# Splitting the first loads, moving block 1's attention ahead of half a projection, and merging two stores at the end of a linear-attention and gated-FFN kernel

## The chip, the cores and the metric

The kernel runs on one core of a Trainium2 chip. The metric is the device time of one execution in microseconds (us), lower is better. The profile of one execution gives a span, from its first to its last instruction, about 2 us shorter than the time. PE is TensorE (the matmul engine), DVE is VectorE, ACT is ScalarE, POOL is GpSimd and SP is SyncE.

## The reference

Linear attention with a decay per head over blocks, then a gated feed-forward layer, in float32. Cut to what matters:

```python
# q, k, v: (4 batches, 8 heads, 768 positions, 64), lam: (8,)
for b in range(nb):                                    # blocks of positions
    intra = einsum('bhic,bhjc->bhij', qb, kb) * Dmask  # scores, decayed and causal
    intra = einsum('bhij,bhjd->bhid', intra, vb)
    inter = einsum('bhid,bhde->bhie', qb * lam_pow, kv_state)
    out[:, :, sl] = intra + inter
    kv_state = lam_block * kv_state + einsum('bhsd,bhse->bhde', kb * rev_pow, vb)
x = out.transpose(0, 2, 1, 3).reshape(3072, 512)
gate = 1 / (1 + exp(-(x @ w_gate)))                    # w_gate, w_val: (512, 1536)
return (gate * (x @ w_val)) @ w_out                    # w_out: (1536, 512)
```

## The kernel before

The kernel works through six blocks of 128 positions, each with all four batches. A block has three parts:

- Attention: transposes of k and q; scores (`sp`); mask products on VectorE (`MT`); the part from the state (`piece_i`) and the value part (`piece_a`), which add up in `op`; copies of these to `XT`; and the update of the state from k with its decays (`KD`, on ScalarE) and v.
- Gate/value: 12 tiles of 128 columns, each with four gate matmuls (`gp`) and four value matmuls (`vp`).
- Output projection (`po`): 12 matmuls over the 12 tiles, for each batch.

The attention of the next block is threaded into the matmul stream of the block that is running. All inputs are float32 and become bfloat16 on the way in; GpSimd issues those loads, one after the other. These are the lines that the change touches:

```python
    # first loads, block 0 (batches 0, 1 of k come by another way)
    load(0, "q", 0, 2)
    load(0, "k", 2, 4)
    load(0, "q", 2, 4)
    load(0, "v", 0, 2)
    load(0, "v", 2, 4)
    load_gv(0, 1); load_gv(1, 2); load_gv(2, 4); load_gv(4, 6)   # gate and value weights by tiles
    # ... cut: tables of decays
    load_gv(6, 8); load_gv(8, 12)
    load(1, "k", 0, 2); load(1, "q", 0, 2)
    load_wo(0, 256)                        # output weights, columns 0 to 255, all 12 row tiles
    load(1, "k", 2, 4); load(1, "q", 2, 4)
    load_wo(256, 512)
    load(1, "v")
    load(2, "kq")
```

(The statements joined by semicolons stand on lines of their own in the kernel.) Block 0's projection runs in two halves of 256 columns, with block 1's attention between the half projections:

```python
    behind[10] = [trans(1, 0)]                          # behind gate tile 10 of block 0
    behind[11] = [pair(piece_s, 1, 0), m_(1, 0)]
    # ...
    after = {(0, 0): [m_(1, 1)], (0, 1): [kd(1, 0), trans(1, 1)],
             (0, 2): [pair(piece_s, 1, 1), m_(1, 2), kd(1, 2)],
             (0, 3): [pair(piece_c, 0, 0), pair(piece_c, 0, 1), m_(1, 3)],
             (1, 0): [kd(1, 4)], (1, 1): [kd(1, 6)], (1, 2): [att(1)]}
    for j in range(2):
        for tt in range(B):
            po(0, tt, *after.get((j, tt), []), c=(256 * j, 256 * (j + 1)))
    # ... the last projection of the kernel (last block, last batch):
                po(n, tt, c=(0, 256))
                po(n, tt, c=(256, 384), eng=nc.vector)
                po(n, tt, c=(384, 512))
```

Each `po` ends with a copy out of PSUM (ScalarE, or VectorE where `eng` says so) and a store that SyncE issues.

## Time and profile before

| | before |
|---|---|
| time, median of the first 3 runs | 229.35 us (229.12 to 229.72) |
| span of the profiled run | 227.2 us |
| PE busy | 218.9 us (96%) |
| first gate matmul starts | 15.85 us |
| first projection matmul starts | 38.65 us |
| first gate matmul of block 1 | 54.09 us |

Busy time by stretches of the kernel before: the stretch in us and its length, then busy us and number of instructions of each engine, the granted clock, the DMA share and GB/s.

```profile
core 0: us, PE busy (x) PEld busy (x) DVE busy (x) ACT busy (x) POOL busy (x), PEclk, DMA share, GB/s
...
15.42:38.65 23.23, 22.55 (x132) 10.56 (x129) 10.25 (x16) 11.52 (x23) 13.47 (x14) 1.00 1.62 193
38.65:54.09 15.44, 15.27 (x260) 13.14 (x257) 9.40 (x18) 9.04 (x26) 4.64 (x5) 1.00 2.18 167
54.09:88.85 34.76, 34.76 (x275) 16.80 (x273) 17.34 (x35) 15.90 (x36) 13.89 (x17) 1.00 1.42 166
```

From 54.09 us on PE is full (34.76 of 34.76 us), so the change can act only on what lies ahead of that, and on the last store. PE is full at its rate too: matmuls of 512 columns start 0.216 us apart. That is what the Trainium skill gives in "TensorE: Matmul & The Clock Gate", section "Back-to-back issue gap", as the isolated gap of a warm array (512/2.4 + 2.5 ns = 216 ns).

PE's waits of 0.3 us and more between 12 and 60 us in the kernel before: who waited for whom, us in total, times, longest.

```profile
PE gp L336 <- ACT XT L421: 0.4, 1, 0.4
PE vp L342 <- DMA WV<-in_moe_w_val_dram: 0.3, 1, 0.3
```

How block 1's attention lies in the stream before is shown by PE's timeline: start, duration, line, operation, output and inputs, number.

```profile
46.57 4.10 PE L358 MATMUL po<-WO,ht 128*128 128x256 bf16 x36
50.61 0.64 PE L285 MATMUL op<-QS,Sb 64*64 64x128 bf16 x32
51.18 1.08 PE L296 MATMUL op<-MT,vb 128*64 128x128 bf16 x32
52.09 0.74 PE L314 MATMUL cp<-vb,kd 128*64 128x64 bf16 x32
52.77 1.48 PE L358 MATMUL po<-WO,ht 128*128 128x256 bf16 x12
54.09 1.03 PE L336 MATMUL gp<-XT,WG 128*128 128x512 bf16 x4
...
57.55 1.03 PE L336 MATMUL gp<-XT,WG 128*128 128x512 bf16 x4
```

The state part (50.61), the value part (51.18) and the state update (52.09) follow one another without a gap, because 36 projection matmuls, 4 us, stand between the update of block 0's state and them; VectorE has done its mask products by then. The last half projection (52.77) covers the copies to `XT` that the first gate matmul of block 1 (54.09, "gate 1" from here on) needs. The line at 57.55 is tile 2 of block 1's gates, counted from 0.

The end: ScalarE's last copy, and SyncE's last stores (its line merges four).

```profile
223.31 0.27 ACT L361 COPY ob<-po 128x128 f32<-128x128 f32 x1 [0.97 <-PE po L358]
```

```profile
221.27 2.88 SPq L350 DMA_DIRECT2D out_dram<-ob  x4
```

The last copy ends at 223.58, the span at 227.17.

The trace also has every load's landing on its semaphore. The ones that matter (us, last of the 16 engines): v of block 0's batches 2, 3 at 14.24, first half of the output weights 38.34, q of block 1's batches 2, 3 41.84, second half of the output weights 45.84, v of block 1 49.16.

### The profile page before, as it was taken

Reading aid. Unit: us, or ns where it says so; the run is one execution under the profiler, and the core shown is the slowest. Engines: PE = TensorE matmul, PEld = TensorE weight load, DVE = VectorE, ACT = ScalarE, POOL = GpSimd, SP = SyncE. Lnnn points to the kernel's source line nnn. Section 1 sums busy time; section 2 is a strip of 40 time slices with the busy share of each in tenths; the row PEclk is TensorE's granted clock in tenths of the full one; section 3 lists DMA queues with packets and bytes.
Section 4 is the critical chain, followed back from the end, with each engine's and each line's share of the span. In section 5 each row is a group of like instructions: output and inputs, shape, how many; then the busy total and the mean of one; then the engine's idle time right before and its main releaser. Section 6 shows DMA issues by size and latency. Waiting matters only on the chain.

```text
span 227.2 us, 4266 instructions
## 1 busy us (share of the span) xinstructions
PE 218.9 (96%) x1725; PEld 111.2 (49%) x1725; DVE 101.8 (45%) x186; ACT 101.2 (45%) x217; POOL 58.1 (26%) x73
## 2 busy tenths in 40 slices
PE   6789999999999999999999999999999999999993
PEld 2444436887444644444644444644444544444452
DVE  4764435547378610488420388430378400334200
ACT  5777433763328723348523338532422342433221
POOL 7997545600192039005800030000000000000000
PEclk9999999999999999999999999999999999999999
DMA  7999999999999929993992959012100012100022
GB/s 114 149 173 202 203 175 182 187 158 142 277 154 159 190 76 151 207 186 61 149 171 97 217 42 66 3 46 92 46 3 0 3 46 92 46 0 3 0 92 94
DMA packets 104708, 25.31 MB, mean 111 GB/s; under 512 B 94065, under 2 KB 101745, under 8 KB 104689
## 3 DMA queue, kind: packets, MB, share of 16 engines
q0 software_dynamic: 81760, 13.90, 78.8%
q1 hardware_dynamic: 22464, 11.01, 19.3%
q8 instruction: 13, 0.21, 0.4%
q10 hardware_dynamic: 464, 0.14, 0.4%
q14 instruction: 7, 0.05, 0.1%
HBM read 28.32 MB, written 6.29 MB: 152 GB/s over the span
## 4 chain that ended last, share of the span: by engine, by line
PE 84%; DMA 9%; POOL 4%; ACT 1%; issue 1%; POOLq 0%
PE po L358 27%; PE vp L342 24%; PE gp L336 24%; DMA WV<-in_moe_w_val_dram 6%; DMA vb<-in_v_dram 3%; PE sp L266 2%; PE op L296 2%; PE op L285 1%; PE cp L314 1%; POOL WV L105 1%; POOL WG L104 1%; POOL qb L92 1%; POOL vb L92 1%; ACT kd L120 1%; POOL kb L92 0%
## 5 line engine op out<-in xcount | busy, mean ns | idle before, releaser
L345 DVE TENSOR_TENSOR ht<-sg,vp 128x512 bf16<-128x512 bf16 x72 | 49.5, 687 | 96.9 <-PE vp L342 95.2
L336 PE MATMUL gp<-XT,WG 128*128 128x512 bf16 x288 | 74.0, 379 | 0.4 <-ACT XT L421 0.4
L342 PE MATMUL vp<-XT,WV 128*128 128x512 bf16 x288 | 73.9, 379 | 0.3 <-DMA WV<-in_moe_w_val_dram 0.3
L339 ACT ACTIVATE sg<-gp 128x512 bf16<-128x512 f32 x72 | 43.0, 597 | 65.6 <-PE gp L336 63.2
L358 PE MATMUL po<-WO,ht 128*128 128x512 bf16 (+2 forms) x360 | 64.1, 337 | 0.0
L358 PEld LDWEIGHTS <-ht 128*128 128x128 bf16 x360 | 33.5, 98 | 27.9
L342 PEld LDWEIGHTS <-WV 128*128 128x128 bf16 x288 | 28.0, 98 | 34.7 <-DMA WV<-in_moe_w_val_dram 1.2
L336 PEld LDWEIGHTS <-WG 128*128 128x128 bf16 x288 | 27.5, 98 | 32.7 <-issue 0.3
L361 ACT COPY ob<-po 128x512 f32<-128x512 f32 (+2 forms) x29 | 14.7, 507 | 46.4 <-PE po L358 46.4
L274 DVE TENSOR_TENSOR MT<-sp,mask 128x512 bf16<-128x512 f32 x48 | 30.6, 683 | 2.0 <-PE sp L266 2.0
L120 ACT ACTIVATE kd<-kb,kds 128x128 bf16<-128x128 bf16 (+1 forms) x72 | 23.8, 402 | 0.0
L443 POOL COPY gates<-kt 128x1 bf16<-128x1 bf16 x4 | 1.2, 304 | 52.1 <-DMA kt<-kb 52.1
L306 ACT CAST XT<-op 128x512 bf16<-128x512 f32 x21 | 10.9, 597 | 5.6 <-PE op L296 5.6
L92 POOL DMA_DIRECT2D vb<-in_v_dram x7 | 10.9, 1564 | 2.7 <-DMA kb<-in_k_dram 1.0
L323 DVE SCALAR_TENSOR_TENSOR Sb<-Sb,dec,cp 128x128 bf16<-128x128 bf16 x32 | 8.6, 342 | 3.3 <-PE cp L314 3.3
L98 POOL DMA_DIRECT2D kb<-in_k_dram x10 | 8.8, 892 | 3.7 <-DMA WO<-in_moe_w_out_dram 2.7
L98 POOL DMA_DIRECT2D qb<-in_q_dram x10 | 8.9, 906 | 2.1 <-DMA WG<-in_moe_w_gate_dram 1.7
L371 PE MATMUL zps<-Sb 128*128 128x512 bf16 x21 | 7.5, 482 | 1.5 <-DVE Sb L147 1.5
L92 POOL DMA_DIRECT2D qb<-in_q_dram x7 | 8.4, 1201 | 1.1 <-POOLq L560 0.8
L92 POOL DMA_DIRECT2D kb<-in_k_dram x6 | 7.0, 1158 | 0.7 <-DMA WG<-in_moe_w_gate_dram 0.7
L296 PE MATMUL op<-MT,vb 128*64 128x128 bf16 x184 | 6.5, 221 | 0.0
L296 PEld LDWEIGHTS <-vb 128*64 128x64 bf16 x184 | 5.3, 110 | 1.3 <-issue 0.4
(55 smaller groups left out, 79.9 us busy)
## 6 DMA issues: line engine op xcount, KB each, us to landing
out_dram<-ob SPq DMA_DIRECT2D x23, 256.0 KB, 2.0
vb<-in_v_dram POOLq DMA_DIRECT2D x5, 512.0 KB, 7.1
qb<-in_q_dram POOLq DMA_DIRECT2D x7, 256.0 KB, 7.5
kb<-in_k_dram POOLq DMA_DIRECT2D x6, 256.0 KB, 8.0
WO<-in_moe_w_out_dram POOLq DMA_DIRECT2D x2, 768.0 KB, 15.5
kb<-in_k_dram POOLq DMA_DIRECT2D x10, 128.0 KB, 9.5
qb<-in_q_dram POOLq DMA_DIRECT2D x10, 128.0 KB, 10.0
WG<-in_moe_w_gate_dram POOLq DMA_DIRECT2D x3, 256.0 KB, 8.3
```

The lines of the kernel that those rows point to most:

```text
L92: nc.gpsimd.dma_start(out=T_[c, n][:, b0:nat], in_=src[b0:nat, :, sl, :].rearrange("b h s d -> s (b h) d"))
L98: nc.gpsimd.dma_start(out=T_[c, n][:, m:b1, u::2, :], in_=src[m:b1, 1 - u::2, sl, :].rearrange("b h s d -> s (b h) d"))
L120: nc.scalar.mul(KD[n][:, at, i, :], T_["k", n][:, at, i, :], kds[:, h:h + 1])
L274: nc.vector.tensor_tensor(out=MT[n, b][:, u], in0=SP[n, b][u], in1=(mask if n else mask0)[:, 1 - u if swapped(n, b) else u], op=ALU.mult)
L296: nc.tensor.matmul(OP[n, b][rows_of(w), hp, :], lhsT=T_["v", n][:, b, h, :], rhs=MT[n, b][:, slot(n, b, h) % 2, hp, :], start=(n == 0 and ...
L306: (e.tensor_copy if e is nc.vector else e.copy)(XT[n][:, :, b, :], OP[n, b])
L336: nc.tensor.matmul(gp, lhsT=WG[:, mt, fs], rhs=x[:, mt, :], start=(mt == 0), stop=(mt == NMT - 1))
L339: nc.scalar.activation(sg, gp, AF.Sigmoid)
L342: nc.tensor.matmul(vp, lhsT=WV[:, mt, fs], rhs=x[:, mt, :], start=(mt == 0), stop=(mt == NMT - 1))
L345: nc.vector.tensor_mul(HT[n, ft], sg, vp)
L358: nc.tensor.matmul(po[:, :c1 - c0], lhsT=HT[n, ft][:, tt * 128:(tt + 1) * 128], rhs=WO[:, ft, c0:c1], start=(ft == 0), stop=(ft == NFT - 1))
L361: (eng.copy if eng is nc.scalar else eng.tensor_copy)(o, po[:, :c1 - c0])
```

## The change

The intent: let the scores of block 0's batches 2 and 3 start as soon as each batch's q is there; keep the weights arriving in step with the gate tiles; bring v of block 1 ahead of the second half of the output weights, so that attention 1 can run early and this half's projection moves into gate/value 1; and have one store fewer at the end. The core of the diff:

```diff
-    load(0, "q", 2, 4)
+    load(0, "q", 2, 3)
+    load(0, "q", 3, 4)
     load(0, "v", 0, 2)
-    load(0, "v", 2, 4)
-    load_gv(0, 1)
-    load_gv(1, 2)
-    load_gv(2, 4)
+    load(0, "v", 2, 3)
+    load(0, "v", 3, 4)
+    for ft in range(4):
+        load_gv(ft, ft + 1)
 ... (transposes may take a PSUM buffer of the other pool; so does block 1's op)
-    t_("k", 0, [2, 3])
-    e_k(0, [2, 3], parts=2)
+    for b in range(2, 4):
+        t_("k", 0, [b], ps_ff, "ff")
+    e_k(0, [2])
     piece_s(0, [1])
     piece_m(0, 1)
-    zeros(2)
     t_("q", 0, [2])
     e_q(0, [2], nc.scalar)
+    e_k(0, [3])
+    zeros(2)
     t_("q", 0, [3])
-    e_q(0, [3], nc.vector)
+    e_q(0, [3], nc.scalar)
 ... (scores of batches 2 and 3 one by one, other filler matmuls, XT of batch 2 on VectorE)
     load_gv(6, 8)
-    load_gv(8, 12)
+    nc.gpsimd.dma_start(out=WG[:, :, 8 * 128:], in_=wg_r[:, :, 8 * 128:])
+    for ft in (8, 10):
+        fs = slice(ft * 128, (ft + 2) * 128)
+        nc.gpsimd.dma_start(out=WV[:, :, fs], in_=wv_r[:, :, fs])
 ...
     load(1, "q", 2, 4)
+    load(1, "v", 0, 2)
+    load(1, "v", 2, 4)
     load_wo(256, 512)
-    load(1, "v")
     load(2, "kq")
 ...
-    behind[10] = [trans(1, 0)]
-    behind[11] = [pair(piece_s, 1, 0), m_(1, 0)]
+    behind[10] = [trans(1, 0), kd(1, 0, 2, parts=[0])]
+    behind[11] = [pair(piece_s, 1, 0), m_(1, 0), kd(1, 2, 4, parts=[0])]
 ... (the table "after" and its loop go)
+    po(0, 0, m_(1, 1), kd(1, 4, 6, parts=[0]), c=cols[0])
+    po(0, 1, pair(piece_c, 0, 0), pair(piece_c, 0, 1), kd(1, 6, 8, parts=[0]), c=cols[0])
+    po(0, 2, trans(1, 1), c=cols[0])
+    po(0, 3, pair(piece_s, 1, 1), m_(1, 2), m_(1, 3), kd(1, 0, 8, parts=[1]), att(1), c=cols[0])
 ...
             gv(n, ft, *more[ft])
+            if (n, ft) == (1, 1):
+                for tt in range(B):
+                    po(0, tt, c=cols[1])
 ...
-                po(n, tt, c=(0, 256))
-                po(n, tt, c=(256, 384), eng=nc.vector)
+                po(n, tt, c=(0, 384), eng=nc.vector)
                 po(n, tt, c=(384, 512))
```

So it has three parts: the front (loads and prologue), the middle (attention 1 early), and the end (two stores for three).

More of the change, by code (lines that the diff above doesn't have):

```diff
@@ L113, in make_kd, with piece_kd @@
         KD[n] = kdp.tile([128, B, H, D], BF16, tag="kd", name="kd")
-    def piece_kd(n, hs):
+    def piece_kd(n, hs, parts=(0, 1)):
         for h in hs:
-            for bs in ((0, B),) if n == 0 else ((0, NB2), (NB2, B)):
+            for bs in ((0, B),) if n == 0 else [((0, NB2), (NB2, B))[i] for i in parts]:
                 at = slice(*bs)
@@ L217, with t_ @@
     tqs, tks = {}, {}
-    def t_(c, n, bs):
-        ps = ps_at.tile([128, len(bs), HP, C], BF16, name="t" + c, tag="ps")
+    def t_(c, n, bs, pool=ps_at, tag="ps"):
+        ps = pool.tile([128, len(bs), HP, C], BF16, name="t" + c, tag=tag)
         for i, b in enumerate(bs):
@@ L279, in piece_i @@
         for b in range(B):
-            OP[n, b] = ps_at.tile([128, HP, C], FP32, name="op", tag="ps")
+            p, t = (ps_ff, "ff") if n == 1 and b < B - 1 else (ps_at, "ps")
+            OP[n, b] = p.tile([128, HP, C], FP32, name="op", tag=t)
         for i in range(NB2):
@@ L391 @@
     piece_m(0, 0)
-    t_("k", 0, [2, 3])
-    e_k(0, [2, 3], parts=2)
+    for b in range(2, 4):
+        t_("k", 0, [b], ps_ff, "ff")
+    e_k(0, [2])
     piece_s(0, [1])
     piece_m(0, 1)
-    zeros(2)
     t_("q", 0, [2])
     e_q(0, [2], nc.scalar)
+    e_k(0, [3])
+    zeros(2)
     t_("q", 0, [3])
-    e_q(0, [3], nc.vector)
+    e_q(0, [3], nc.scalar)
     nc.scalar.preload_act_table_set("sigmoid_and_others")
+    piece_s(0, [2])
+    piece_m(0, 2)
+    zeros(3)
+    piece_s(0, [3])
+    piece_m(0, 3)
     zeros(1)
-    for b in range(2, 4):
-        piece_s(0, [b])
-        piece_m(0, b)
+    for b in range(3):
+        piece_a(0, [b])
+        piece_x(0, [b], nc.vector if b == 2 else nc.scalar)
     zeros(2)
-    for b in range(2):
-        piece_a(0, [b])
-        piece_x(0, [b], nc.scalar)
-    zeros(3)
-    piece_a(0, [2])
-    piece_x(0, [2], nc.scalar)
-    zeros(1)
     ops = [ps_at.tile([128, HP // 2, C], FP32, name="op", tag="ps") for _ in range(2)]
@@ L488, in att, with kd @@
         return go
-    def kd(n, h0):
-        return lambda: piece_kd(n, [h0, h0 + 1])
+    def kd(n, h0, h1=None, **kw):
+        return lambda: piece_kd(n, range(h0, h1 or h0 + 2), **kw)
     behind = {ft: [] for ft in range(NFT)}
@@ L498 @@
     behind[3].append(lambda: make_mask(1))
-    behind[10] = [trans(1, 0)]
-    behind[11] = [pair(piece_s, 1, 0), m_(1, 0)]
+    behind[10] = [trans(1, 0), kd(1, 0, 2, parts=[0])]
+    behind[11] = [pair(piece_s, 1, 0), m_(1, 0), kd(1, 2, 4, parts=[0])]
     for ft in range(NFT):
         gv(0, ft, *behind[ft])
-    after = {(0, 0): [m_(1, 1)], (0, 1): [kd(1, 0), trans(1, 1)],
-             (0, 2): [pair(piece_s, 1, 1), m_(1, 2), kd(1, 2)],
-             (0, 3): [pair(piece_c, 0, 0), pair(piece_c, 0, 1), m_(1, 3)],
-             (1, 0): [kd(1, 4)], (1, 1): [kd(1, 6)], (1, 2): [att(1)]}
-    for j in range(2):
-        for tt in range(B):
-            po(0, tt, *after.get((j, tt), []), c=(256 * j, 256 * (j + 1)))
+    cols = [(256 * j, 256 * j + 256) for j in range(2)]
+    po(0, 0, m_(1, 1), kd(1, 4, 6, parts=[0]), c=cols[0])
+    po(0, 1, pair(piece_c, 0, 0), pair(piece_c, 0, 1), kd(1, 6, 8, parts=[0]), c=cols[0])
+    po(0, 2, trans(1, 1), c=cols[0])
+    po(0, 3, pair(piece_s, 1, 1), m_(1, 2), m_(1, 3), kd(1, 0, 8, parts=[1]), att(1), c=cols[0])
     for n in range(1, NSTEP):
```

## The prediction

> **What bounds the kernel now.** From 54.09 us on the tensor engine (PE) is full: busy time by stages gives 34.76 of 34.76 us, 34.60 of 34.60. Only the start can change: the prologue to 15.42 us, block 0's gate/value stage (22.55 of 23.23 us busy), block 0's projection with block 1's attention (15.27 of 15.44), and the last store.
>
> Up to 38 us a second limit lies close behind: the GpSimd load queue, which lands loads in issue order and never runs dry. Landings in the trace: q2,3 10.89, v2,3 14.24, output weights' first half 38.34, q of block 1's batches 2,3 41.84, second half 45.84, block 1's v 49.16. Per 128 KB (as written) attention tensors take 0.84 us, weights 0.73, so splitting moves few landings. (Narrow rows going slower agrees with the Trainium skill, "DMA: Bandwidth & Descriptors", "Why small descriptors are slow".)
>
> **Gains.**
> - Prologue: batch 2's q lands at about 10.0 (estimate), both q evictions leave VectorE, and its eight mask products (pitch 0.60 us) end by 14.2 instead of 14.90. The last value product then waits for v at 14.24: first gate matmul at 15.2 instead of 15.85.
> - Gate/value 0: the waits of tile 2 (0.4 us) and tile 11 (0.5 us) for value weights go; one at tile 4 stays (landing 23.37). PE would be ready for the projection at 37.9 instead of 38.65. But the output weights' first half has the same bytes ahead of it and lands near 38.3 again: projection starts at 38.4. Only 0.25 survives.
> - Tail: 384+128 columns instead of 256+128+128, same PE time, one store fewer. SyncE issued the last store 0.24 us after its eviction, normally 0.02: -0.2 us.
>
> **Cost.** Before, half projections cover block 1's mask products and decays. Now the attention follows its own scores at once. From the start T of the scores of batches 2,3: scores 0.57, state part 0.57, three value parts 0.75, so PE is at T+1.9; VectorE's last product ends at T+0.43+3x0.60+0.69 = T+2.9 (0.43 from scores at 43.98, product at 44.41). PE idles 1.05 us, does the last value part and the state update (to T+3.85), then waits for batch 3's XT copy, the second behind the products (T+4.15). ScalarE's eight decays (pitch 0.29 us) and two copies end at T+3.9. Gate 1 starts at T+4.2 with 2.7 us of PE work done: 1.5 us idle, against 0.3 in this region before. The moved half projection's weights (about 49.1) come before its place (about 53).
>
> **Sum.** -0.25 + 1.2 - 0.2 = +0.7 us: predicted 230.0 us, against 229.35; 8 in 10 between 228.9 and 230.9. Chances: faster by over 2% 0.01, within 2% 0.97, slower by over 2% 0.02.
>
> **What would show it.** Timeline: first gate matmul at 15.2. Waits: the first projection matmul waits about 0.4 us for output weights, near 38.4; tile 11 doesn't wait. PE idles about 1 us before the last value part of block 1 while VectorE's products run without gaps, then 0.4 us before gate 1, on XT. Block 1's gate tile 2 starts at 58.5 to 58.8 instead of 57.7.
>
> **What would make it wrong.** Output weights landing before 38 us (about 229.6 then); VectorE's products standing earlier against PE; PE falling to its cold clock in the prologue, with fewer filler matmuls; more loads waiting for one of the eight semaphores that the queue rotates through, so that it runs dry; block 1's v landing later than about 45 us, stopping the attention.

## More of the kernel before

Block 0's projection follows its last scores without a wait:

```profile
38.10 0.62 PE L266 MATMUL sp<-QS,KS 64*128 64x128 bf16 x16
38.65 0.83 PE L358 MATMUL po<-WO,ht 128*128 128x256 bf16 x6
```

## The result, and the profile after

The changed kernel took 229.50 us (median of 4 runs, 229.42 to 229.61), the kernel before 229.45 in the same rounds: ratio 1.0003, 95% interval 0.9986 to 1.002. The time is the same. (A ratio is the mean time of one kernel's fast runs over that of the other's of the same rounds, so not quite the ratio of the medians quoted.) It lies inside the predicted range, 0.5 us under the predicted value. That the total is the same hides two large moves. (The profiled run of the kernel before took 229.03 us, at the fast end of its runs, and that of the changed kernel 229.50; so the spans of the profiles below differ by 0.46 us where the medians differ by 0.05.)

Busy time by the same stretches, changed kernel:

```profile
15.42:38.65 23.23, 22.39 (x126) 10.50 (x128) 10.30 (x17) 12.19 (x25) 15.76 (x18) 1.00 1.67 190
38.65:54.09 15.44, 13.82 (x227) 10.42 (x228) 10.80 (x23) 8.16 (x21) 5.78 (x6) 1.00 2.19 168
54.09:88.85 34.76, 34.55 (x294) 18.94 (x296) 15.44 (x29) 15.82 (x37) 14.41 (x17) 1.00 1.50 165
```

PE is busy only 13.82 of the 15.44 us in which it was busy 15.27 before. PE's waits of 0.3 us and more between 12 and 60 us:

```profile
PE po L360 <- DMA WO<-in_moe_w_out_dram: 0.8, 1, 0.8
PE op L298 <- DVE MT L275: 0.8, 1, 0.8
PE vp L344 <- DMA WV<-in_moe_w_val_dram: 0.4, 1, 0.4
PE gp L338 <- ACT XT L423: 0.4, 1, 0.4
PE gp L338 <- DVE XT L308: 0.3, 1, 0.3
```

Two lines of 0.8 us are new: the projection waits for the output weights, and the value part for VectorE's mask products; so is the wait of gate 1 for the `XT` copy. The wait for value weights is not the old one: before it stood in tile 8 of block 0, now it stands in tile 4, whose value weights land at 23.70 (23.37 before). The places are in PE's timeline, first where the projection starts:

```profile
37.69 0.62 PE L267 MATMUL sp<-QS,KS 64*128 64x128 bf16 x16
39.14 0.38 PE L360 MATMUL po<-WO,ht 128*128 128x256 bf16 x2 [0.82 <-DMA WO<-in_moe_w_out_dram]
```

The scores are done at 38.3, but the weights land at 39.10. Then the attention of block 1:

```profile
46.65 0.64 PE L287 MATMUL op<-QS,Sb 64*64 64x128 bf16 x32
47.22 1.07 PE L298 MATMUL op<-MT,vb 128*64 128x128 bf16 x24
49.07 0.41 PE L298 MATMUL op<-MT,vb 128*64 128x128 bf16 x8 [0.78 <-DVE MT L275]
49.29 0.70 PE L316 MATMUL cp<-vb,kd 128*64 128x64 bf16 x32
50.27 1.04 PE L338 MATMUL gp<-XT,WG 128*128 128x512 bf16 x3 [0.28 <-DVE XT L308]
...
58.97 0.81 PE L338 MATMUL gp<-XT,WG 128*128 128x512 bf16 x2
```

VectorE in the same stretch:

```profile
46.53 2.48 DVE L275 TENSOR_TENSOR MT<-sp,mask 128x512 bf16<-128x512 f32 x4 [0.94 <-PE sp L267]
48.93 1.28 DVE L308 CAST XT<-op 128x512 bf16<-128x512 f32 x2
```

The state part and 24 of the 32 value matmuls run while VectorE is still at its four products (46.53 to 49.01); the last eight wait until 49.07. Gate 1 starts at 50.27, after the second `XT` copy (48.93 + 1.28 = 50.21). The half projections that covered this before are now elsewhere. Tile 2 of block 1's gates (counted from 0) starts at 58.97, against 57.55 before: the head of the kernel has become 1.42 us longer.

The end, changed kernel:

```profile
224.70 0.27 ACT L363 COPY ob<-po 128x128 f32<-128x128 f32 x1 [2.03 <-PE po L360]
```

```profile
222.70 2.73 SPq L352 DMA_DIRECT2D out_dram<-ob  x3
```

The last copy ends at 224.97, 1.39 us later than before, but the span ends at 227.63, only 0.46 us later: from the last copy to the end it took 3.59 us before and takes 2.66 us now. So in these two profiles about 1.4 us were lost in the head and 0.93 us won at the end.

### The profile page after: what moved, and what is told of

Its sections match the earlier page's. It is cut to its first block, busy times and chain, and to the rows that moved or that the text cites. A ratio compares the mean times of both kernels' runs of the same rounds, so it can differ in the third digit from the quotient of the medians.

```text
span 227.6 us, 4221 instructions
## 1 busy us (share of the span) xinstructions
PE 217.2 (95%) x1688; PEld 110.4 (49%) x1712; DVE 102.3 (45%) x186; ACT 100.9 (44%) x216; POOL 61.6 (27%) x79
## 3 DMA queue, kind: packets, MB, share of 16 engines
q0 software_dynamic: 83392, 13.90, 79.7%
## 4 chain that ended last, share of the span: by engine, by line
PE 79%; POOL 9%; DMA 7%; issue 2%; DVE 2%; ACT 0%; POOLq 0%
PE po L360 28%; PE vp L344 23%; PE gp L338 22%; DMA WO<-in_moe_w_out_dram 7%; PE sp L267 2%; POOL WG L104 2%; POOL WV L105 2%; PE op L298 2%; POOL qb L92 1%; POOL vb L92 1%; DVE MT L275 1%; PE op L287 1%; POOL kb L92 1%; PE cp L316 1%; POOL WV L434 1%
## 5 line engine op out<-in xcount | busy, mean ns | idle before, releaser
L338 PE MATMUL gp<-XT,WG 128*128 128x512 bf16 x273 | 71.9, 380 | 1.5 <-issue 0.5
L360 PE MATMUL po<-WO,ht 128*128 128x512 bf16 (+3 forms) x343 | 63.6, 342 | 1.1 <-DMA WO<-in_moe_w_out_dram 0.8
L449 POOL COPY gates<-kt 128x1 bf16<-128x1 bf16 x4 | 0.7, 186 | 53.4 <-DMA kt<-kb 53.4
L92 POOL DMA_DIRECT2D vb<-in_v_dram x9 | 11.9, 1331 | 2.4 <-issue 1.3
L308 ACT CAST XT<-op 128x512 bf16<-128x512 f32 x20 | 10.3, 596 | 4.8 <-PE op L298 4.7
L98 POOL DMA_DIRECT2D qb<-in_q_dram x10 | 8.9, 911 | 2.2 <-DMA WG<-in_moe_w_gate_dram 1.7
L92 POOL DMA_DIRECT2D qb<-in_q_dram x8 | 9.1, 1135 | 0.8 <-POOLq L566 0.8
L373 PE MATMUL zps<-Sb 128*128 128x512 bf16 x18 | 6.8, 507 | 1.7 <-DVE Sb L147 1.5
```

Source lines behind the costliest of these rows:

```text
L92: nc.gpsimd.dma_start(out=T_[c, n][:, b0:nat], in_=src[b0:nat, :, sl, :].rearrange("b h s d -> s (b h) d"))
L98: nc.gpsimd.dma_start(out=T_[c, n][:, m:b1, u::2, :], in_=src[m:b1, 1 - u::2, sl, :].rearrange("b h s d -> s (b h) d"))
L308: (e.tensor_copy if e is nc.vector else e.copy)(XT[n][:, :, b, :], OP[n, b])
L338: nc.tensor.matmul(gp, lhsT=WG[:, mt, fs], rhs=x[:, mt, :], start=(mt == 0), stop=(mt == NMT - 1))
L360: nc.tensor.matmul(po[:, :c1 - c0], lhsT=HT[n, ft][:, tt * 128:(tt + 1) * 128], rhs=WO[:, ft, c0:c1], start=(ft == 0), stop=(ft == NFT - 1))
```

## The experiments

All kernels gave correct results. Each was timed in five rounds, beside the kernel before on the same chip. Where a run alters one thing, its sources stand as a short diff.

### The end alone, and everything but the end

e1_tail_only is the kernel before with the new end (the diff below); e2_old_tail is the changed kernel with the old end (the same diff undone):

```diff
-                po(n, tt, c=(0, 256))
-                po(n, tt, c=(256, 384), eng=nc.vector)
+                po(n, tt, c=(0, 384), eng=nc.vector)
                 po(n, tt, c=(384, 512))
```

> The kernel before with only the changed end (384 + 128 columns). Theory (parts that cancel): the end was worth 0.9 us, because the last eviction ends at 223.58 of a span of 227.17 before (3.59 us to go) and at 224.97 of 227.63 in the changed kernel (2.66 us to go): 228.5 us, and 2.6 to 2.7 us from the last eviction to the end in the profile. Rival (as predicted): the end is worth 0.2 us, and the rest of the 0.9 us is chance in when the last store lands: 229.2 us and about 3.3 us to go.

> The changed kernel with the old end (256 + 128 + 128 columns). Theory: loses the 0.9 us again, 230.4 us, so the head of the change costs about 1.0 to 1.3 us. Rival (end worth 0.2 us): 229.7 us.

Measured: e1_tail_only 228.34 us against 229.33 (ratio 0.9959, interval 0.9947 to 0.9972); e2_old_tail 230.38 us (ratio 1.0045, 1.0033 to 1.0058). The end is worth about 1.0 us, and the rest costs about 1.0 us in time. The prediction's 0.2 us for the end falls.

### The front alone, and the middle alone

e3_front_only has the changed loads and prologue with the old middle and end; e4_middle_only has the changed middle with the old front and end. Their diffs are the parts of the change's own diff.

> Only the prologue and the single loads up to gate/value 0 (q, v, first gate tiles, last value weights split), with the middle and the end of the kernel before. Theory (the projection is held by the load queue): first gate matmul near 15.4 as in the changed kernel, but the first projection matmul stays where the first half of the output weights lands, near 39.1 (38.34 before), so 0.0 to 0.6 us slower than before in spite of the earlier start. Rival (prologue gain is kept): projection starts at 38.2, 0.4 to 0.6 us faster than before. Second rival for the later landing (39.10 against 38.34): chance of one execution, then it lands near 38.3 here and the time equals that of before.

> Only the middle: v ahead of the second half of the output weights, block 1's attention right behind its own scores, the second half projection inside gate/value 1; prologue and end as before. Theory (exposed VectorE chain): tensor engine idle about 0.8 us before the last value part and 0.4 us before gate 1, 0.9 to 1.2 us slower than before, about 230.5 us, block 1's gate tile 2 at 58.7 to 58.9 against 57.7. Rival (the loss in the changed kernel comes from its later loads, not from the order): no more than 0.3 us slower.

Measured: e3_front_only 229.80 us (ratio 1.0021, 1.0007 to 1.0034), e4_middle_only 230.47 us (ratio 1.0043, 1.0031 to 1.0056), both against 229.33. In e3_front_only the first gate matmul starts at 15.34 instead of 15.85, and yet the kernel is slower. PE's waits between 30 and 62 us, e3_front_only:

```profile
PE tq L224 <- DMA qb<-in_q_dram: 0.7, 1, 0.7
PE po L359 <- DMA WO<-in_moe_w_out_dram: 0.6, 1, 0.6
```

The projection starts at 38.91, when the output weights have landed (38.87), and then PE waits for q of block 1's batches 2, 3, which lands at 42.69 (41.84 before) while the old middle wants it right behind the second half projection. So the prologue's half microsecond is lost to the first load that has to be waited for, and more than lost because that load lands later. In e4_middle_only, in the same window:

```profile
PE op L297 <- DVE MT L274: 0.8, 1, 0.8
PE gp L337 <- DVE XT L307: 0.3, 1, 0.3
PE vp L343 <- DMA WV<-in_moe_w_val_dram: 0.3, 1, 0.3
```

The third is the wait of the kernel before. The first two are the two exposed waits of the changed kernel, without its front: 1.1 us together, and the time is 0.43% or 1.0 us longer. Front and middle alone cost 0.5 and 1.0 us, together (e2_old_tail) 1.0 and not 1.5. A part of this is plain in the waits: the changed middle has no wait for q at 42.6, since it asks for the transposes one half projection later.

The landings of the loads in these and in later runs, read from the trace's semaphore records (us, last of 16):

| run | v of batches 2, 3 | output weights, first half | q of block 1, batches 2, 3 |
|---|---|---|---|
| before | 14.24 | 38.34 | 41.84 |
| e1_tail_only (old loads) | 14.33 | 38.58 | 42.10 |
| e4_middle_only (old front) | 14.38 | 38.49 | 42.13 |
| changed kernel | 14.56 | 39.10 | 42.58 |
| e2_old_tail (new front) | 14.47 | 39.04 | 42.64 |
| e3_front_only (new front) | 14.52 | 38.87 | 42.69 |
| e8_wide_weights (q and v split, weights wide) | 14.44 | 38.47 | 41.90 |

With the new front the weights land at 39.00 in the mean of three, with the old one at 38.47: 0.53 us later for the same bytes. It is not chance: of the later runs that load these weights in one piece, e10_seven_more_stores (old front) has 38.48, e6_scores_early and e9_one_more_store (new front) have 39.11 and 39.01.

### The projection's wait, taken away

e5_wo_rows loads the first half of the output weights as two loads of six row tiles. The first six matmuls of a projection need only the first of them:

```diff
-    load_wo(0, 256)
+    for ft in (0, 6):
+        nc.gpsimd.dma_start(out=WO[:, ft:ft + 6, 0:256], in_=wo_r[:, ft:ft + 6, 0:256])
```

> The changed kernel with the first half of the output weights (256 columns) loaded as two loads of six of its twelve row tiles each; same bytes in the same place of the queue. Theory (the projection is held by that landing): the first six row tiles land near 37.2, the first projection matmul starts near 38.3 when the scores are done, instead of 39.14, the seventh matmul of it waits a little for the second load (39.1), and all that follows moves up by 0.5 to 0.7 us: about 228.9 us. Rival (the load queue as a whole is late, q of block 1 at 42.6 as well, and its transposes stand behind three half projections anyway): 0.2 us or less.

Measured: 228.79 us against 229.38 (ratio 0.9975, 0.996 to 0.999), where the changed kernel had 1.0003. The two loads land at 36.93 and 38.90. PE's timeline, e5_wo_rows:

```profile
37.69 0.62 PE L267 MATMUL sp<-QS,KS 64*128 64x128 bf16 x16
38.24 1.30 PE L360 MATMUL po<-WO,ht 128*128 128x256 bf16 x10
```

The projection follows the scores at once, 0.90 us earlier than in the changed kernel, and the last copy of the kernel ends 0.85 us earlier (224.12 against 224.97); by the two ratios the time is about 0.6 us shorter. The landing of that one load was what held it. The scores themselves start at 37.69 in both, though e5_wo_rows starts its first gate matmul 0.32 us earlier (15.06 against 15.38): both wait in tile 4 for value weights that land at 23.69 and 23.70, which takes that lead back.

### The exposed products, covered again

e6_scores_early moves block 1's transposes one half projection earlier and the scores ahead of the last half projection; e7_both joins this with the edit before.

```diff
-    po(0, 1, pair(piece_c, 0, 0), pair(piece_c, 0, 1), kd(1, 6, 8, parts=[0]), c=cols[0])
-    po(0, 2, trans(1, 1), c=cols[0])
-    po(0, 3, pair(piece_s, 1, 1), m_(1, 2), m_(1, 3), kd(1, 0, 8, parts=[1]), att(1), c=cols[0])
+    po(0, 1, pair(piece_c, 0, 0), pair(piece_c, 0, 1), trans(1, 1), kd(1, 6, 8, parts=[0]), c=cols[0])
+    po(0, 2, pair(piece_s, 1, 1), m_(1, 2), m_(1, 3), kd(1, 0, 4, parts=[1]), c=cols[0])
+    po(0, 3, kd(1, 4, 8, parts=[1]), att(1), c=cols[0])
```

> The changed kernel with block 1's transposes of batches 2, 3 one half projection earlier and their scores ahead of the last half projection, so that this covers VectorE's four mask products. Theory (the loss in the middle is the exposed VectorE chain): the two tensor waits (0.78 us for the products, 0.3 to 0.4 for the XT copy) shrink to 0.1 to 0.3 together, 0.8 to 1.0 us faster than the changed kernel, about 228.6 us. Rival (the eight decays on ScalarE and the XT copies behind them are the limit, not the products): no more than 0.3 us faster.

> The two edits before together. If they act on different waits their gains add, save that the transposes now stand so early that they wait for q of batches 2, 3 (landing near 42.6): 1.1 to 1.4 us faster than the changed kernel, 228.1 to 228.4 us, so about level with the kernel before with the new end alone (228.34).

Measured: e6_scores_early 228.92 us against 229.38 (ratio 0.9983, 0.9969 to 0.9997), e7_both 229.11 us (0.9983, 0.9968 to 0.9999). PE's waits between 36 and 60 us, e6_scores_early:

```profile
PE po L360 <- DMA WO<-in_moe_w_out_dram: 0.6, 1, 0.6
PE gp L338 <- DVE XT L308: 0.4, 1, 0.4
PE op L287 <- ACT ob L363: 0.3, 1, 0.3
```

The wait for the mask products is gone, so they were the limit there. But not all of the gain comes: PE now waits 0.3 us for ScalarE's copy of the last half projection (the state part takes that PSUM buffer), and gate 1 still waits 0.4 us for the `XT` copy. The last copy of the kernel ends at 224.59, 0.38 us earlier than in the changed kernel, not 0.8 to 1.0.

The gains of e5_wo_rows and e6_scores_early do not add. Gate 1 starts at 49.88 in e7_both and at 49.89 in e6_scores_early. One line of PE's waits in e7_both (14 to 60 us) is absent in e6_scores_early:

```profile
PE tq L224 <- DMA qb<-in_q_dram: 0.3, 1, 0.3
```

The projection starts at 38.63 against 39.15 in e6_scores_early, and the transposes of q then meet their load (landing 42.80): they start at 42.94 in e7_both and at 42.95 in e6_scores_early, so the lead is gone there. The load queue gives the pace again, only at another load. The expectation had named this wait, and had still taken most of the sum.

### Which loads delay the queue

e8_wide_weights puts the wide loads of weights back (gate tiles 2 and 3 together, value tiles 8 to 11 together), and keeps q and v split.

> The changed kernel with the weights of gate tiles 2, 3 and the value weights of tiles 8 to 11 loaded wide as before; q and v of batches 2, 3 stay split. Theory (each extra load costs the queue about 0.1 us): the first half of the output weights lands near 38.7 (38.34, 38.58, 38.49 with all loads wide; 39.10, 39.04, 38.87 with all split), and the time is 0.2 to 0.4 us shorter, because the projection waits for that load alone. Rival (the split q and v cost it all): it lands at 39.0 again, same time or slower by the waits of tiles 2 and 11.

Measured: the first half of the output weights lands at 38.47, the same as with all loads wide. By this one profile it is the three more loads of weights that cost 0.5 us of queue, not the two more of q and v. The delay is there before the output weights' turn: the last value weights land at 31.56 in the changed kernel, at 31.13 in e8_wide_weights and at 31.01 in the kernel before.

The profile pages show a difference between the two kinds of split. The load queue moves the same 13.90 MB in 81760 packets before, 83392 in the changed kernel and 81808 in e8_wide_weights. The three further loads that e8_wide_weights keeps bring 16 packets each. Each of the three splits of weights, which are by columns, brings 512 more on top, since it cuts every row of its tiles in two; q and v are split by batches and their rows stay whole. The landings fit this. For each 128 KB, as written, the load of gate tiles 8 to 11 took 0.64 us (2.55 us for four tiles), the two loads of value tiles 8 to 11 about 0.67 (1.36 and 1.31 us), single tiles 0.73; two batches of q in one load took 0.85 and one batch 0.84 to 0.88. An estimate from these figures for the three splits of weights is 0.4 us. e5_wo_rows cut a load of weights by rows: 16 packets more (83408), and the last part landed no later (38.90 against 39.10). A run that varies the width of the rows alone was not made.

The time of e8_wide_weights, though, is 229.60 us (ratio 1.0013, 0.9998 to 1.0029), no shorter. Of PE's waits in e8_wide_weights, the line for value weights:

```profile
PE vp L345 <- DMA WV<-in_moe_w_val_dram: 0.7, 3, 0.4
```

That line has three waits of 0.7 us in total, where the changed kernel had one of 0.4: by the starts of the gate matmuls they lie in tiles 1, 2 and 8 (tile 8 is the first that needs the wide load of tiles 8 to 11, which the prediction calls tile 11), and PE reaches the projection at 38.78, after the weights are there. So the projection starts only 0.36 us earlier than in the changed kernel, since waits that the split had removed returned, and the last copy ends 0.35 us earlier (224.62). That is in the profiled run, the fastest of its five (229.36 us); the five times together do not show it, and why is not shown.

### The end taken apart

Why two stores instead of three save a microsecond is seen in SyncE's records. After the last store SyncE goes through a fixed list of nine waits, 0.06 us each; the eight semaphores of its stores take turns, so the number of stores decides which one the last store has. Before it is the one that the list names second (107), in the changed kernel the one that it names last (118). SyncE's records after the last copy, in order, from the kernel before and from the changed kernel (us; what each waits for):

```
before:  223.82 last store issued, on 107    | 224.20 wait 106 | 225.84 107 (landed 225.82) | 225.90 109 | 225.96 111 | 226.02 114 | 226.08 115 | 226.14 116 | 226.20 117 | 226.26 118
changed: 225.06 last store issued, on 118    | 225.89 wait 106 | 225.97 107 | 226.04 109 | 226.10 111 | 226.17 114 | 226.23 115 | 226.29 116 | 226.53 117 | 226.75 118 (landed 226.73)
```

Before, seven waits that were long satisfied come after the landing; in the changed kernel they pass while the store is under way. There is a second effect: in both kernels SyncE's 80th record of the trace comes 0.78 to 0.83 us after the issue of the store ahead of it, where it is 0.38 to 0.39 us after other stores at the end. Before, this pause falls between the last two stores and makes the last one late; in the changed kernel it falls behind the last store. All fourteen traces have this pause at the 80th record, and in all of them a DMA of the kind that the profile calls "instruction", 8192 bytes, starts 0.62 to 0.89 us after that record; so it does in e10_seven_more_stores below, where the 80th record comes at 217.03. That ties the pause to the place in SyncE's stream, not to the store.

Two runs move the turn of the semaphores without touching the end. e9_one_more_store is the changed kernel with one store of block 0, far from the end, cut in two. e10_seven_more_stores is the kernel before with block 0's four stores cut into eleven. The edit of the first:

```diff
-            more[3].extend([lambda tt=tt: store(0, tt) for tt in range(B)])
+            more[3].extend([lambda: store(0, 0, 0, 256), lambda: store(0, 0, 256, 512)])
+            more[3].extend([lambda tt=tt: store(0, tt) for tt in range(1, B)])
```

> The changed kernel with one of block 0's four stores, in the middle of the span, cut in two, so that SyncE issues one store more and the last store of the kernel falls on the same semaphore as in the kernel before, which the closing chain of waits names second of nine, not last. Theory (half of what the end gained is the place of that semaphore): eight closing waits of 0.06 us each follow the landing instead of preceding it: 0.4 to 0.5 us slower than the changed kernel, about 229.9 us; time from the last eviction to the end 3.1 us instead of 2.66. Rival (only the number and size of the last stores matter): no difference.

> The kernel before with block 0's four stores cut into eleven, so that its last store falls on the semaphore that the closing chain names last. Theory: 0.4 to 0.5 us faster than before, about 228.9 us, and about 3.1 us from the last eviction to the end instead of 3.59; the last store is still issued late (0.24 us after its eviction) since the three last stores stay. Rival (only the last stores matter): same as before; second rival: seven stores more cost time, slower than before.

Measured, from the traces (us, each column from the end of the one before it, all from the last copy's end):

| run | last stores | semaphore | copy to issue | issue to landing | landing to end | sum |
|---|---|---|---|---|---|---|
| before | 256, 128, 128 | 107 | 0.24 | 2.00 | 1.35 | 3.59 |
| e2_old_tail | 256, 128, 128 | 107 | 0.24 | 2.09 | 1.34 | 3.67 |
| changed kernel | 384, 128 | 118 | 0.09 | 1.67 | 0.90 | 2.66 |
| e1_tail_only | 384, 128 | 118 | 0.09 | 1.76 | 0.90 | 2.75 |
| e9_one_more_store | 384, 128 | 107 | 0.52 | 1.80 | 1.33 | 3.65 |
| e10_seven_more_stores | 256, 128, 128 | 118 | 0.03 | 2.19 | 0.92 | 3.14 |

One more store in the middle of the kernel puts all of the gain back: e9_one_more_store took 230.83 us against 229.19 (ratio 1.0058, 1.0044 to 1.0072). It lost more than the 0.4 to 0.5 us expected, because it also brought the pause in front of the last store (0.52 instead of 0.09 us). e10_seven_more_stores shows the 0.43 us from landing to end and the missing pause in its trace, 0.45 us less from copy to end, but its time of 229.13 us (ratio 0.9991, 0.9977 to 1.0005) does not show it clearly: its copy ended 0.16 us later, and the interval holds both -0.5 us and 0. So the 0.93 us of the end, in the profiled runs, are 0.15 us of issue, 0.33 us of landing (1.66 to 1.83 us in the nine profiles with two last stores, on either semaphore, 1.86 to 2.19 in the five with three) and 0.45 us of closing waits. Why three last stores land more slowly than two, and what SyncE does in the pause, is not shown.

### A version that beats both

If the order of the kernel before covers attention 1, if the early loads are kept, and if no load is asked for before it lands, the prologue should count. e11_old_middle_rows has the changed front and end, the old middle, both halves of the output weights in two loads each, and the transposes of k and q a half projection apart:

```diff
-    after = {(0, 0): [m_(1, 1)], (0, 1): [kd(1, 0), trans(1, 1)],
-             (0, 2): [pair(piece_s, 1, 1), m_(1, 2), kd(1, 2)],
-             (0, 3): [pair(piece_c, 0, 0), pair(piece_c, 0, 1), m_(1, 3)],
+    after = {(0, 0): [m_(1, 1)], (0, 1): [trk, kd(1, 0)], (0, 2): [trq, kd(1, 2)],
+             (0, 3): [pair(piece_s, 1, 1), m_(1, 2), pair(piece_c, 0, 0), pair(piece_c, 0, 1), m_(1, 3)],
```

> A version meant to beat both: the changed front and end, the order of the kernel before in the middle (attention behind seven of eight half projections, so VectorE's products are covered), both halves of the output weights loaded as two loads of six row tiles, and the transposes of k and q of block 1's batches 2, 3 set apart by a half projection, so that neither stands where its load is late. Theory (prologue gain counts once no landing holds it, and the middle needs no idle): projection starts at 38.3, no tensor wait over 0.2 us from there to gate 1, gate 1 at 53.4 to 53.7 (54.09 before), and with the end worth 0.9 to 1.0 us 227.5 to 227.9 us. Rival (the load queue moves the wait on, to the second half of the weights or to v at about 50): 228.3 us or more, level with the new end alone.

Measured: 228.18 us against 229.19 (ratio 0.9953, 0.994 to 0.9965), no better than the new end alone (0.9959). The projection started at 38.31 as expected, but the update of block 0's state, placed right behind the scores, took 1.00 us from its start to the next projection matmul instead of 0.62, and gate 1 started at 54.18. e12_update_earlier moves it:

```diff
-             (0, 1): [trk, kd(1, 0)], (0, 2): [trq, kd(1, 2)],
-             (0, 3): [pair(piece_s, 1, 1), m_(1, 2), pair(piece_c, 0, 0), pair(piece_c, 0, 1), m_(1, 3)],
+             (0, 1): [trk, pair(piece_c, 0, 0), pair(piece_c, 0, 1), kd(1, 0)],
+             (0, 2): [trq, kd(1, 2)], (0, 3): [pair(piece_s, 1, 1), m_(1, 2), m_(1, 3)],
```

> The version of the run before it, with block 0's state update two half projections earlier (behind the transposes of k), because there it stood behind the scores and waited 0.5 us for a PSUM buffer that VectorE's first products had to free. Theory: that wait goes, gate 1 starts near 53.8 instead of 54.18, 227.7 to 227.9 us. Rival: the buffers move the wait to the scores or to the attention, no change, 228.2 us.

Measured: 227.74 us against 229.20 (ratio 0.9932, 0.9917 to 0.9947). PE's timeline around attention 1, to be held against that of the kernel before:

```profile
50.09 0.64 PE L287 MATMUL op<-QS,Sb 64*64 64x128 bf16 x32
50.66 1.08 PE L298 MATMUL op<-MT,vb 128*64 128x128 bf16 x32
51.57 0.67 PE L316 MATMUL cp<-vb,kd 128*64 128x64 bf16 x32
52.18 1.48 PE L360 MATMUL po<-WO,ht 128*128 128x256 bf16 x12
53.50 1.03 PE L338 MATMUL gp<-XT,WG 128*128 128x512 bf16 x3
```

The same row of parts stands there without a gap, and gate 1 starts at 53.50, 0.59 us ahead of 54.09. The kernel's last copy ends at 222.95 (223.58 before). This is the fastest version, 0.7% faster than the kernel before, which the changed kernel equals.

## Why the prediction was right or wrong

- **The result: the same time.** Right: 229.50 us measured, 230.0 predicted, range 228.9 to 230.9. But the sum was right with two terms that were wrong in opposite directions by nearly the same amount (0.74 and 0.73 us in the profiles): that they cancelled was luck.
- **"First gate matmul at 15.2 instead of 15.85."** Nearly right: 15.38 in the changed kernel, 15.34 in e3_front_only. The term of v was a little off: batch 3's v landed at 14.56, not at 14.24. That v is the limit there is seen in all ten runs with the new front: the first gate matmul starts 0.81 to 0.86 us after that landing, wherever it lies between 14.20 and 14.79. Little of this gain reaches the projection, because tile 4 then waits for its value weights (landing 23.70, not 23.37): PE was ready for the projection at 38.3, not at 37.9. Of the two waits that the prediction saw removed in this stage, only one cost PE time before, 0.33 us, in tile 8 (not 11); at tile 2 the weight loader waited 0.36 us, and PE's matmuls came 0.05 us late.
- **"The output weights' first half has the same bytes ahead of it and lands near 38.3 again: projection starts at 38.4."** The mechanism was right (e5_wo_rows takes that wait away and its last copy ends 0.85 us earlier); the size was off. It landed at 39.10 and the projection started at 39.14. The step that failed is "splitting moves few landings": the three more loads of weights delayed the queue by about 0.5 us (e8_wide_weights against the three runs with the new front). The prediction took one rate, 0.73 us per 128 KB, for all weights; that is the rate of single tiles, and the wide load of four tiles ran at 0.64. So the start of the projection became +0.49 us, not -0.25.
- **"1.5 us idle, against 0.3 in this region before."** Right in kind, slightly too large: 0.78 us for the mask products and about 0.3 to 0.4 us for the `XT` copy, in the places named. From the start of the projection to block 1's gate tile 2 it took 19.83 us against 18.90, +0.93 where +1.2 was predicted. e4_middle_only shows it without the front.
- **Block 1's gate tile 2 starting "at 58.5 to 58.8".** 58.97, late by the late projection: +1.42 us against 57.55 on the same timeline.
- **"Tail: ... -0.2 us."** Wrong size: 0.93 us in the profiles and 1.0 us in time (e1_tail_only). The term counted only the late issue of the last store, which gave 0.15. It left out the faster landing of the last store (0.33) and the closing list of waits, which the changed count of stores moved out of the way (0.45).
- **The sum.** Predicted -0.25 + 1.2 - 0.2. Measured in the profiles +0.49 + 0.93 - 0.93, with the span 0.46 us longer.

What stays open: whether the narrower rows of the split weights are the whole of the half microsecond (one profile without them, and packet counts, speak for it), why e8_wide_weights is no faster in time, and what the pause of SyncE is.

## What to carry to other kernels

A time that does not move can be a loss and a gain of the same size: undo the parts one by one before calling a change neutral. When loads arrive in one queue just ahead of their use, an earlier start is worth nothing until the next load that lands late is split by what is needed first, or asked for later; and each such cure shows the next load. Look too at what a split does to the rows of a load: here splits by columns doubled its packets and cost queue time, splits by batch or by row tiles did not. Work taken out of the matmul stream for one reason may have been covering another engine's chain, so before moving it, look at what runs beside it. A change at the end of a kernel should be timed alone, since the number of stores can decide how the closing waits fall.

## What the Trainium skill lacked or had wrong

- "TensorE: Matmul & The Clock Gate", section "Back-to-back issue gap", gives 131 ns per matmul of 512 columns and 81 ns per matmul of 128 columns as the rate of a real stream of weight loads and matmuls. Here such streams ran at 216 ns and 56 ns (gate/value tiles, and the last 128-column projections), which is what that section's formula for the isolated gap gives.
- "DMA: Bandwidth & Descriptors" says under "Why small descriptors are slow" that small descriptors carry a fixed overhead each. The runs agree: attention tensors, written in packets of 128 bytes, took 0.84 us per 128 KB, single weight tiles (256 bytes) 0.73, and the load of four tiles (1024 bytes) 0.64. What splitting costs in a queue that is never empty is not given there: three more loads of weights, 1536 packets more for the same bytes, delayed what came behind by about 0.5 us.
- No page that I read has the closing list: SyncE waits for its store semaphores in a fixed order, 0.06 us each, so a last store on the second of nine ends the kernel 1.33 to 1.35 us after its landing, and on the last 0.90 to 0.93 us.
- "Runtime: NRT & Kernel Launch", section "Instruction fetch mechanics", calls the cost of crossing a block of instructions "mostly hidden". In all fourteen runs SyncE's 80th record came 0.78 to 0.83 us after the store ahead of it, instead of the usual 0.38 to 0.39, and in one of them this put off the last store by 0.43 us (0.52 instead of 0.09 us after its copy). An "instruction" DMA of 8192 bytes starts 0.62 to 0.89 us after that record; whether fetching is the cause of the pause, no run shows.
